# The forward transform over the rows in four 64x64 quarters of TensorE, even and odd rows apart

## The chip, the cores and the metric

The kernel runs on one core of a Trainium2 chip. The metric is the device time of one execution in microseconds; the median of several runs is compared. A profile is one execution recorded by the hardware profiler, with the start and the end of every instruction on each engine: TensorE (PE, with its weight loads as PEld), VectorE (DVE), ScalarE (ACT), GpSimd (POOL) and SyncE (SP), which here only issues transfers. Times within a profile are counted from the start of its span.

## What is computed

```python
x = A_x                                   # 1 x 2048 x 1024
xn = _layernorm(x, axis=-1)
X = rfft2(xn) * (w_r + 1j * w_i)          # w_r, w_i: 2048 x 513
s = irfft2(X, (2048, 1024))
h = silu(einsum("bsd,df->bsf", xn, w1))   # w1: 1024 x 3584
g = silu(einsum("bsf,fd->bsd", h, w2))    # w2: 3584 x 1024
return x + s * g
```

A layer norm feeds two branches. One is a feed-forward layer with two large products. The other multiplies the two-dimensional Fourier transform of the normed rows with a complex filter and transforms back. Both meet in the last line.

## The kernel before

Every product with f32 data is made of three f16 products: each operand is split into a high and a low half, and high x high, high x low and low x high are summed in PSUM.

TensorE has a first stage, the product with w1 (`mm1`, tiles `pa`, 112 groups of 24 matmuls of 512 columns), and a second, the product with w2 (`mm2`, tiles `pb`, 56 groups of 42 in seven combined products, so that fewer are needed than by the plain rule). Between these groups the code puts the matmuls of the Fourier branch:

- `fa` (in `fd_gen`): the transform over the 1024 columns of a row block. VectorE combines its parts (`bfly`), makes four-point sums over four row blocks (`Rb`, `Rd`, `Ro`) and stores the result, split into halves, to the DRAM tensors `vd`.
- `fx` (in `f_gen`): the transform over the 2048 rows s. Before the change it has 16 units u = 4q + j: q is one of four residue classes of the frequency over s, j one of four blocks of 128 column frequencies. `mat(u)` multiplies data `vq` (128 rows, four row classes c, real and imaginary parts) with constants `kq`: for each c and each of the three half products one matmul of 256 columns and two of 128. ScalarE copies half of the sums from PSUM (`xc`), VectorE adds and subtracts (`xb`, `xd`, then `radix4` to `X`), multiplies with the filter (`T`, from the tiles `wq` of w_r and w_i, which ScalarE scales first), makes the first inverse sums (`yb`, `yd`, `Z`), and `high_z` and `low_z` split Z into halves `zq` that go to the DRAM tensors `zd`.
- `iu` and `id` (in `i_gen`): the inverse transforms, on 64-row halves of TensorE. They read `zd` as `zt`.
- The frequencies 0 and 512 over the columns go a way of their own (`xsv`, `edge_gen`, `zp`). `wmax_gen` reads all of w_r and w_i once for a scale `zs`, and `w2max_gen` does so for w2.

The order is written by generators. After each group of the first or second stage `work()` takes a step of the weights' queue `wq`, in three of four cases one of the queue `xq` (the two maxima, then the edge), and up to three steps of the queue `bg`, which holds the Fourier branch: it goes on as long as a model of VectorE's time (`clock`, summed by `meter` from sizes) is no more than `LEAD` = 1 us ahead of that of TensorE. The filter's turn comes when the maxima are done (`switch`). `defer(n, ...)` puts a transfer off by n groups. The order within an engine is fixed by this; the engines run freely against each other and wait on semaphores. SP issues loads (`vq`, `wq`, and the `ht` of the second stage) in one order, POOL's queue the loads of w2 (`jr`) and `kq` and most stores.

PSUM has two buffers for the Fourier branch (pool `pt`, tag `ft`) and four for the large products (`pf`). `vq` and `kq` have two buffers each in the pool of the filter, `xc` has one.

## Time and profile before

| | |
|---|---|
| time, median of 3 runs | 1247.46 us (1245.87 to 1251.45) |
| the profiled execution's own time | 1247.57 us |
| its span | 1245.8 us |
| granted clock of TensorE, mean | 0.997 |
| matmuls, columns transform `fx` | 576, first at 573.3 us, last ones at 810 |
| inverse, `iu` | 768, first at 871.7 us, last at 1150.3 |
| DMA | 296.88 MB, 238 GB/s mean |

A line of the profile's groups reads: source line, engine, operation, the tiles written and read, their shapes, the count, then busy time, mean duration in ns of one, and the engine's idle time just ahead of them with what ended it. A line of the timeline has start and duration in us. A line of the waits has who waited, for whom, the total in us, how often, and the longest. Under DMA stand bytes of one transfer and the median time from issue to landing.

### The profile page before, as it was taken

Reading aid. Unit: us, or ns where it says so; the run is one execution under the profiler, and the core shown is the slowest. Engines: PE = TensorE matmul, PEld = TensorE weight load, DVE = VectorE, ACT = ScalarE, POOL = GpSimd, SP = SyncE. Lnnn points to the kernel's source line nnn. Section 1 sums busy time; section 2 is a strip of 40 time slices with the busy share of each in tenths; the row PEclk is TensorE's granted clock in tenths of the full one; section 3 lists DMA queues with packets and bytes.
Section 4 is the critical chain, followed back from the end, with each engine's and each line's share of the span. In section 5 each row is a group of like instructions: output and inputs, shape, how many; then the busy total and the mean of one; then the engine's idle time right before and its main releaser. Section 6 shows DMA issues by size and latency. Waiting matters only on the chain. (4 is left out here: it accounts for less than half of the span.)

```text
span 1245.8 us, 20664 instructions
## 1 busy us (share of the span) xinstructions
PE 1225.4 (98%) x7759; PEld 621.0 (50%) x7759; DVE 1018.9 (82%) x2056; ACT 499.4 (40%) x672; POOL 321.1 (26%) x526
## 2 busy tenths in 40 slices
PE   8999999999999999999999999999999998999997
...
DVE  6678999998988998565958799894895886895985
...
GB/s 239 124 184 192 126 247 171 192 189 159 156 237 229 236 282 332 254 228 180 196 274 229 264 250 245 295 146 360 234 216 301 207 322 375 248 330 240 231 297 317
DMA packets 161733, 296.88 MB, mean 238 GB/s; under 512 B 32048, under 2 KB 84912, under 8 KB 161120
## 3 DMA queue, kind: packets, MB, share of 16 engines
...
q8 instruction: 61, 1.00, 0.3%
...
q10 hardware_dynamic: 144, 0.13, 0.0%
...
## 5 line engine op out<-in xcount | busy, mean ns | idle before, releaser
L432 PE MATMUL pa<-xnT,w 128*128 128x512 f16 x2688 | 585.1, 379 | 2.6 <-DVE xnT L686 1.7
L432 PEld LDWEIGHTS <-w 128*128 128x128 f16 x2688 | 262.3, 98 | 313.4 <-issue 2.0
L510 PE MATMUL pb<-w,ht 128*128 128x512 f16 (+1 forms) x798 | 300.3, 376 | 0.4 <-DMA ht<-hd_one 0.4
L511 PE MATMUL pb<-w,ht 128*128 128x512 f16 (+1 forms) x798 | 300.0, 376 | 0.0
L512 PE MATMUL pb<-w,ht 128*128 128x512 f16 (+1 forms) x798 | 300.0, 376 | 0.0
L512 PEld LDWEIGHTS <-ht 128*128 128x128 f16 x798 | 78.2, 98 | 91.5 <-issue 0.8
L510 PEld LDWEIGHTS <-ht 128*128 128x128 f16 x798 | 78.3, 98 | 90.3 <-issue 0.8
L511 PEld LDWEIGHTS <-ht 128*128 128x128 f16 x798 | 78.3, 98 | 87.2 <-issue 0.6
L441 ACT ACTIVATE h<-pa,s 128x512 f32<-128x512 f32 x112 | 75.2, 677 | 76.7 <-PE pa L432 70.0
L231 DVE SCALAR_TENSOR_TENSOR w<-jr,sc,w 128x512 f16<-128x512 f32 x98 | 71.9, 745 | 33.9 <-ACT w L228 33.8
L228 ACT ACTIVATE w<-jr,sc 128x512 f16<-128x512 f32 x98 | 68.6, 714 | 76.7 <-DMA jr<-in_B_w_dram 69.6
L388 POOL DMA_DIRECT2D jr<-in_B_w_dram x56 | 36.7, 655 | 226.0 <-issue 162.1
L464 POOL DMA_DIRECT2D hd_sum<-hosum x52 | 38.2, 771 | 183.1 <-DVE hosum L231 116.7
L228 ACT ACTIVATE hosum<-hr,hs 128x1536 f16<-128x1536 f32 x28 | 44.0, 1573 | 88.7 <-DVE hr L471 48.0
L952 ACT ACTIVATE zq<-Z 128x192 f16<-128x192 f32 (+2 forms) x80 | 37.2, 542 | 104.0 <-DVE Z L218 67.4
L228 ACT ACTIVATE hoone<-h,hs 128x2048 f16<-128x2048 f32 x28 | 56.0, 1998 | 53.3 <-DMA hd_one<-hoone 22.7
L231 DVE SCALAR_TENSOR_TENSOR hoone<-h,hs,hoone 128x2048 f16<-128x2048 f32 x28 | 65.6, 2343 | 12.0 <-ACT hoone L228 12.0
L470 DVE TENSOR_TENSOR hr<-h 128x1024 f32<-128x1024 f32 x28 | 34.2, 1220 | 35.3 <-ACT h L441 35.1
L464 POOL DMA_DIRECT2D hd_one<-hoone x52 | 46.0, 884 | 66.1 <-DVE hoone L231 21.1
L231 DVE SCALAR_TENSOR_TENSOR hosum<-hr,hs,hosum 128x1536 f16<-128x1536 f32 x28 | 50.7, 1811 | 3.2 <-ACT hosum L228 3.2
L228 ACT ACTIVATE w<-w1r,rs 128x1024 f16<-128x1024 f32 x28 | 31.8, 1143 | 47.6 <-DVE w L231 26.4
L591 ACT ACTIVATE pl<-pl,c 128x512 f32<-128x512 f32 (+1 forms) x26 | 17.0, 683 | 74.7 <-DVE pl L570 45.6
(215 smaller groups left out, 1798.4 us busy)
## 6 DMA issues: line engine op xcount, KB each, us to landing
jr<-in_B_w_dram POOLq DMA_DIRECT2D x84, 256.0 KB, 7.3
w1r<-in_B_w_dram SPq DMA_DIRECT2D x28, 512.0 KB, 5.9
w2m<-in_B_w_dram SPq DMA_DIRECT2D x28, 512.0 KB, 6.3
...
hd_sum<-hosum POOLq DMA_DIRECT2D x52, 256.0 KB, 4.5
hd_one<-hoone POOLq DMA_DIRECT2D x52, 256.0 KB, 4.5
```

Of the source, the lines that this page charges most:

```text
L228: nc.scalar.activation(hi, raw, AF.Copy, scale=scale)
L231: nc.vector.scalar_tensor_tensor(lo, raw, scale, hi, op0=OP.mult, op1=OP.subtract)
L388: nc.gpsimd.dma_start(raw[n], ws[m][q] if m in ws else w2_block(m, q, 0))
L432: nc.tensor.matmul(ps, w[:, wh, d], xt[:, xh, d], start=(n == 0), stop=(n == 23))
L441: nc.scalar.activation(hq[:, 2 * (c % 2) + f % 2], ps, AF.Silu, scale=s1[:, f:f + 1])
L464: defer(1, lambda k=k, m=m: stores[0].dma_start(hd[m, g][:, :, q].rearrange("f p h s -> f p (h s)"), o[:, k].rearrange("f p h s -> f p (h ...
L470: tt(sums[:, 0:2], hq[:, 0::2], hq[:, 1::2], op=OP.subtract)
L510: nc.tensor.matmul(ps, hh[:, 0], w[:, 0], start=first, stop=False)
L511: nc.tensor.matmul(ps, hh[:, 0], w[:, 1], start=False, stop=False)
L512: nc.tensor.matmul(ps, hh[:, 1], w[:, 0], start=False, stop=last)
L591: nc.scalar.activation(o, o, AF.Silu, scale=c2)
L952: nc.scalar.activation(o[0], z, AF.Copy)
```

## The change

The transform over s now works on the two halves of its symmetric matrix. The residue classes q and q + 2 are taken together (index h), and even and odd rows apart: a unit u has 8 instead of 16 values, and each of its two `mat(u, e)` takes two of the four row classes c. The even rows (b = 0) lie on the first 64 partitions, the odd ones (b = 1) on the others, and each is multiplied with a 64 x 64 block. The four matmuls (b, h) = (0,0), (1,1), (0,1), (1,0) read rows 64b of the array and write columns 64h, so each is one quarter of TensorE, with b in different PSUM banks. `kq` shrinks to half and has one buffer. The sums over even and odd rows, and those between the classes, move to VectorE (`xs`, then two kinds of combination for t = 0 and t = 1, in place of `xb` and `xd` twice).

Column frequencies are sorted by their class of 16 from the first transform on, by the order of the constants `ca` and by the views that `bfly` and the four-point sums use (68 columns for 65 in `bfly`, three more adds per row block in the sums). The split of `Z` then has one or two pieces instead of five and includes the scale `zs`, so ScalarE scales no filter tiles. The filter itself is sorted while `wmax_gen` reads it: five copies on ScalarE for each of 16 blocks, stored to DRAM as `wp` and loaded from there. `zd` is written in 32 stores with runs of 256 bytes. The edge's values take a turn through DRAM (`zpd`).

The queue `xq` gets a step after every group, the edge's loads come 20 groups sooner, and within the filter VectorE's model may be 2 us ahead (`lead`). The diff, cut:

```diff
+    col = np.arange(64)
+    kk = 16 * (col % 4) + col // 4
+    ca = ca[:, :, np.concatenate([kk, 64 + kk])]
...
-    zd = [dp.tile([128, 4, 2, 1024], F16, name=f"zd{c}") for c in range(4)]
...
+    zd = dp.tile([128, 8, 4, 2, 4, 128], F16, name="zd")
...
+    wp = [dp.tile([S, 512], F32, name=f"wp{i}") for i in range(2)]
+    wpv = [t.rearrange("(m2 t m q) k -> q t m m2 k", m2=4, t=2, q=4) for t in wp]
...
-            halves = 2 if name == "pe" and inst.ins[0].ap[0][1] == 64 else 1
+            halves = (2 if inst.ins[0].ap[0][1] == 64 else 1) * (2 if inst.outs[0].ap[0][1] == 64 else 1) if name == "pe" else 1
...
+            for o_, op in ((b, OP.add), (d, OP.subtract)):
+                ov = o_.rearrange("a p r (n l i) -> a n (p r) l i", n=len(parts), i=32)
+                for n, (la, lz, st) in enumerate(parts):
+                    nc.vector.tensor_tensor(ov[:, n], *(rows_[:, k:k + 4, la:lz + 1:st] for k in (0, 4)), op=op)
...
+                t_, o = tl.pop(k - 2), ap.tile([128, 2, 512], F32, name=f"wc{k}", tag="x", bufs=4)
+                nc.vector.tensor_reduce(mt[:, k - 2:k - 1], t_, axis=AX.XY, op=OP.max, apply_absolute_value=True)
+                src = t_.rearrange("m r (i l) -> m r l i", l=16)
+                dst = o.rearrange("m r (g l i) -> m r l g i", g=4, l=4)
+                nc.scalar.activation(o.rearrange("m r (l i) -> m r l i", i=32)[:, :, 0:4], src[:, :, 0:13:4], AF.Copy)
+                for n, (la, st) in enumerate(((3, -1), (13, 1), (5, 1), (11, -1))):
+                    nc.scalar.activation(dst[:, :, n, 1:4], src[:, :, la:la + 3 * st:st], AF.Copy)
+                for i in range(2):
+                    defer(1, lambda o=o, i=i, k=k: stores[0].dma_start(wp[i][128 * k - 256:128 * k - 128, :], o[:, i]))
...
-            t_ = bp.tile([128, 4, 2, 3, 128], F16, name=f"kq{q}", tag="K", bufs=2)
-            nc.gpsimd.dma_start(t_, kf[q])
-            B["k"][q] = t_
+            B["k"][q] = t_ = bp.tile([128, 2, 4, 2, 3, 64], F16, name=f"kq{q}", tag="K", bufs=1)
+            nc.gpsimd.dma_start(t_.rearrange("a p c h t m -> a p (c h t m)"), kf[q])
...
-            t_ = bp.tile([128, 4, 2, 256], F16, name=f"vq{u}", tag="vq", bufs=2)
-            nc.sync.dma_start(t_, vd[j][:, q])
-            B["v"][u] = t_
+            for h in range(2):
+                B["v"][u, h] = t_ = bp.tile([128, 4, 2, 256], F16, name=f"vq{u}_{h}", tag="vq", bufs=2)
+                src = vd[j][:, q + 2 * h].rearrange("(a b) c h k -> b a (c h k)", b=2)
+                for b in range(2):
+                    nc.sync.dma_start(t_[64 * b:64 * b + 64].rearrange("a c h k -> a (c h k)"), src[b])
...
+        def mat(u, e):
+            ps = pt.tile([128, 2, 2, 2, 128], F32, name=f"fx{u}_{e}", tag="ft")
+            k = B["k"][u // 4]
+            for x in range(2):
                 for n, (kh, vh) in enumerate(((0, 0), (0, 1), (1, 0))):
-                    nc.tensor.matmul(o, k[:, c, kh, 1], v[:, c, vh], start=(n == 0), stop=False)
-                    nc.tensor.matmul(ps[:, c, 0], k[:, c, kh, 2], v[:, c, vh, 128:256], start=False, stop=False)
-                    nc.tensor.matmul(ps[:, c, 1], k[:, c, kh, 0], v[:, c, vh, 0:128], start=False, stop=(n == 2))
-            psx[u] = ps
+                    for kind, cols, to in ((1, slice(0, 256), slice(0, 256)), (2, slice(128, 256), slice(0, 128)), (0, slice(0, 128), slice(128, 256))):
+                        for b, h in ((0, 0), (1, 1), (0, 1), (1, 0)):
+                            rows_, out_ = slice(64 * b, 64 * b + 64), slice(64 * h, 64 * h + 64)
+                            o = ps[out_, b, x].rearrange("m r k -> m (r k)")[:, to]
+                            nc.tensor.matmul(o, k[rows_, h, e + 2 * x, kh, kind], B["v"][u, h][rows_, e + 2 * x, vh, cols],
+                                             start=(n == 0 and kind == 1), stop=(n == 2 and kind == 0))
+            psx[u, e] = ps
+
+        def copy(u, e):
+            cps[u, e] = bp.tile([128, 2, 2, 128], F32, name=f"xc{u}_{e}", tag="xc", bufs=2)
...
+            for z, o in by_class(n):
+                stt(o[1], z, zs, o[0], op0=OP.mult, op1=OP.subtract)
+            zs_.pop(n)
+            t_ = zqs.pop(n).rearrange("m h n k -> m (h n) k")
+            for h in range(2):
+                to = zd[64 * t:64 * t + 64, 2 * (q + 2 * h):2 * (q + 2 * h) + 2, :, :, 3 - j].rearrange("m h c r k -> m (h c r) k")
+                defer(1, lambda h=h, to=to: stores[0].dma_start(to, t_[64 * h:64 * h + 64]))
...
+            X = bp.tile([128, 8, 128], F32, name=f"X{n}", tag="X", bufs=2)
+            if n:
+                high_z(n - 1)
+            if t == 0:
+                sd_ = bp.tile([128, 2, 2, 2, 2, 128], F32, name=f"xs{u}", tag="S", bufs=1)
+                for e in range(2):
+                    ps, cpy = psx.pop((u, e))[:, 0], cps.pop((u, e))
+                    for k, op in enumerate((OP.add, OP.subtract)):
+                        tt(sd_[:, k, e], ps, cpy, op=op)
+                if u + 1 < 8:
+                    load_v(u + 1)
+                b = bp.tile([128, 2, 2, 128], F32, name=f"xb{n}", tag="xb", bufs=1)
+                d = bp.tile([128, 2, 2, 128], F32, name=f"xd{n}", tag="xd", bufs=1)
+                tt(b, sd_[:, 0, :, 0], sd_[:, 0, :, 1], op=OP.add)
+                tt(d, sd_[:, 0, :, 0], sd_[:, 0, :, 1], op=OP.subtract)
+                radix4(-1, b, d, X)
+            else:
+                ev = bp.tile([128, 4, 128], F32, name=f"xb{n}", tag="xb", bufs=1)
+                od = bp.tile([128, 4, 128], F32, name=f"xd{n}", tag="xd", bufs=1)
+                pm_ = bp.tile([128, 2, 2, 128], F32, name=f"xp{n}", tag="xp", bufs=1)
+                D = sd_[:, 1]
+                tt(pm_[:, 0], D[:, 1, 0], D[:, 1, 1], op=OP.add)
+                tt(pm_[:, 1], D[:, 1, 0], D[:, 1, 1], op=OP.subtract)
+                tt(ev[:, 0:2], D[:, 0, 0], D[:, 0, 1, ::-1], op=OP.add)
+                tt(ev[:, 2:4], D[:, 0, 0], D[:, 0, 1, ::-1], op=OP.subtract)
+                tt(od[:, 0:2], pm_[:, 1], pm_[:, 0, ::-1], op=OP.add)
+                tt(od[:, 2:4], pm_[:, :, 1], pm_[:, ::-1, 0], op=OP.subtract)
+                b0, b1, d0, d1 = ev[:, 0:4:3], od[:, 0:4:3], ev[:, 2:0:-1], od[:, 1:3]
+                stt(X[:, 0:2], b1, RH, b0, op0=OP.mult, op1=OP.add)
+                stt(X[:, 4:6], b1, -RH, b0, op0=OP.mult, op1=OP.add)
+                stt(X[:, 2:8:5], d1[:, ::-1], RH, d0, op0=OP.mult, op1=OP.add)
+                stt(X[:, 6:2:-3], d1[:, ::-1], -RH, d0, op0=OP.mult, op1=OP.add)
...
+            if u + 1 < 8:
+                mat(u + 1, t)
+                if t and u == 2:
+                    defer(3, lambda: load_k(1))
...
-            if count[0] % 4:
-                slot(xq)
+            slot(xq)
             clock["dve"] = max(clock["dve"], clock["pe"] - 1.0)
             for _ in range(3):
-                if clock["dve"] > clock["pe"] + LEAD or hold[0] or slot(bg) == PAUSE:
+                if clock["dve"] > clock["pe"] + lead[0] or hold[0] or slot(bg) == PAUSE:
...
-            if 44 <= n < 76:
-                load_edge(n - 44)
+            if 24 <= n < 56:
+                load_edge(n - 24)
```

On PE, at the first unit of the filter, before the change; `pa` is a group of the first stage, `kq` the constants and `vq` the data:

```order
L432 MATMUL pa_22_5479<-xnT_670,w_22_4589 128x512
L912 LDWEIGHTS kq_5306
L912 MATMUL fx_5512<-vq_5360,kq_5306 128x256
L913 LDWEIGHTS kq_5306
L913 MATMUL fx_5512<-vq_5360,kq_5306 128x128
L914 LDWEIGHTS kq_5306
L914 MATMUL fx_5512<-vq_5360,kq_5306 128x128
```

And now, where vq_0 and vq_1 are the data of the two classes h, and fx_0 is the tile of e = 0:

```order
L436 MATMUL pa_23_5344<-xnT_490,w_23_4846 128x512
L943 LDWEIGHTS kq_5195
L943 MATMUL fx_0_5375<-vq_0_5232,kq_5195 64x256
L943 LDWEIGHTS kq_5195
L943 MATMUL fx_0_5375<-vq_1_5235,kq_5195 64x256
L943 LDWEIGHTS kq_5195
L943 MATMUL fx_0_5375<-vq_1_5235,kq_5195 64x256
L943 LDWEIGHTS kq_5195
L943 MATMUL fx_0_5375<-vq_0_5232,kq_5195 64x256
L943 LDWEIGHTS kq_5195
L943 MATMUL fx_0_5375<-vq_0_5232,kq_5195 64x128
```

A triple of three full loads and matmuls has become twelve pairs of 64 rows by 64 columns.

On SP, the first loads of the filter, before; `vd` and `w_r`, `w_i` are sources in DRAM:

```order
L892 DMA vq_5434<-vd_76 128x2048
L900 DMA wq_0_5436<-in_A_w_r_dram 64x4x128 x2
L900 DMA wq_1_5439<-in_A_w_i_dram 64x4x128 x2
L892 DMA vq_5551<-vd_77 128x2048
L900 DMA wq_0_5679<-in_A_w_r_dram 64x4x128 x2
L900 DMA wq_1_5682<-in_A_w_i_dram 64x4x128 x2
L892 DMA vq_5699<-vd_78 128x2048
L900 DMA wq_0_5921<-in_A_w_r_dram 64x4x128 x2
L900 DMA wq_1_5924<-in_A_w_i_dram 64x4x128 x2
L892 DMA vq_5934<-vd_75 128x2048
```

And now, from the second filter tile of unit 0 on:

```order
L929 DMA wq_0_5306<-wp_81 64x4x128 x2
L929 DMA wq_1_5309<-wp_82 64x4x128 x2
L921 DMA vq_0_5531<-vd_76 64x2048 x2
L921 DMA vq_1_5534<-vd_76 64x2048 x2
L929 DMA wq_0_5758<-wp_81 64x4x128 x2
L929 DMA wq_1_5761<-wp_82 64x4x128 x2
L929 DMA wq_0_5971<-wp_81 64x4x128 x2
L929 DMA wq_1_5974<-wp_82 64x4x128 x2
L921 DMA vq_0_5986<-vd_77 64x2048 x2
L921 DMA vq_1_5989<-vd_77 64x2048 x2
```

The loads of vq ran two units ahead of their matmuls; now a unit has two tiles of vq, and they are issued when the unit before has been multiplied. On PE, 24 matmuls of `pa` stand between fx_1 of unit 0 and fx_0 of unit 1, 63 or more between the later units, and 84 between unit 3 and unit 4, whose `kq` is the second one. Ahead of the first `fx` stand 2208 matmuls of `pa`, before 2424.

On VectorE, from the sums read out of PSUM to the filter product, one unit, before:

```order
L978 TENSOR_TENSOR xb_6619<-fx_6521,xc_6604 128x512
L979 TENSOR_TENSOR xd_6620<-fx_6521,xc_6604 128x512
L215 TENSOR_TENSOR X_6623<-xb_6619 128x256
L216 TENSOR_TENSOR X_6623<-xb_6619 128x256
L217 TENSOR_TENSOR X_6623<-xd_6620 128x2x128
L218 TENSOR_TENSOR X_6623<-xd_6620 128x2x128
L957 TENSOR_TENSOR zq_6613<-Z_6606,zq_6613 128x8x3x8
L957 TENSOR_TENSOR zq_6613<-Z_6606,zq_6613 128x8x4x8
L957 TENSOR_TENSOR zq_6613<-Z_6606,zq_6613 128x32x8
L957 TENSOR_TENSOR zq_6613<-Z_6606,zq_6613 128x8x3x8
L957 TENSOR_TENSOR zq_6613<-Z_6606,zq_6613 128x8x2x8
L999 TENSOR_TENSOR T_6709<-X_6623,wq_0_6457 128x1024
```

And now:

```order
L1002 TENSOR_TENSOR xs_7542<-fx_0_7210,xc_0_7321 128x512 x2
L1002 TENSOR_TENSOR xs_7542<-fx_1_7386,xc_1_7532 128x512 x2
L1007 TENSOR_TENSOR xb_7553<-xs_7542 128x512
L1008 TENSOR_TENSOR xd_7554<-xs_7542 128x512
L219 TENSOR_TENSOR X_7539<-xb_7553 128x256
L220 TENSOR_TENSOR X_7539<-xb_7553 128x256
L221 TENSOR_TENSOR X_7539<-xd_7554 128x2x128
L222 TENSOR_TENSOR X_7539<-xd_7554 128x2x128
L977 SCALAR_TENSOR_TENSOR zq_7540<-Z_7534,zs,zq_7540 128x1024
L1046 TENSOR_TENSOR T_7656<-X_7539,wq_0_7376 128x1024
L1047 TENSOR_TENSOR T_7658<-X_7539,wq_1_7379 128x1024
```

The second fence is the t = 0 half of a unit now. Ahead of fx_0 of the next unit stand the rows up to X, in the order in which the code was written; its PSUM buffer is the one that the first two xs rows read.

More of the change, by code (lines that the diff above doesn't have):

```diff
@@ L184, in tile_of @@
         return pool.tile(shape, dtype, name=name, tag=tag, bufs=bufs)
-    clock, pace = {"pe": 0.0, "dve": 0.0}, [1.0]
+    clock, pace, lead = {"pe": 0.0, "dve": 0.0}, [1.0], [LEAD]
     COST = {"DVE": ("dve", 0.07, 1.045e-3), "PE": ("pe", 0.0025, 0.4167e-3)}
@@ L837, in fd_gen @@
             o[j] = r.rearrange("a (q r) k -> a q (r k)", r=2)
+            last = j
             yield 3.9
-        high_r(3)
+        high_r(0)
         yield 0.5
-        low_r(3)
+        low_r(0)
         yield 1
@@ L917, in f_gen @@
+        def copy(u, e):
+            cps[u, e] = bp.tile([128, 2, 2, 128], F32, name=f"xc{u}_{e}", tag="xc", bufs=2)
+            nc.scalar.activation(cps[u, e], psx[u, e][:, 1], AF.Copy)
         load_k(0)
-        for n, t_ in enumerate((ones, ident, turn2)):
-            nc.gpsimd.dma_start(t_, pm[:, n])
         yield PAUSE
@@ L964, in f_gen @@
[L964 to L981 removed]
+        tt, stt = nc.vector.tensor_tensor, nc.vector.scalar_tensor_tensor
@@ new lines, in by_class, with high_z @@
+        def by_class(n):
+            src, dst = zs_[n].rearrange("m n (l i) -> m n l i", l=4), zqs[n].rearrange("m h n (l i) -> m h n l i", l=4)
+            for to, k, at in ((0, 4, 0),) if n // 2 % 4 else ((0, 2, 0), (2, 2, 1)):
+                yield src[:, :, at:4:4 // k], [dst[:, h, :, to:to + k] for h in range(2)]
+        def high_z(n):
+            zqs[n] = bp.tile([128, 2, 8, 128], F16, name=f"zq{n}", tag="zq", bufs=2)
+            for z, o in by_class(n):
+                nc.scalar.activation(o[0], z, AF.Copy, scale=zs)
@@ new lines, in f_gen @@
+        mat(0, 0)
+        yield 1
+        mat(0, 1)
+        copy(0, 0)
+        yield 1
+        copy(0, 1)
+        pace[0], lead[0] = 1.05, 2.0
+        for n in range(16):
+            u, t = n // 2, n % 2
+            q, j = u // 4, u % 4
+            X = bp.tile([128, 8, 128], F32, name=f"X{n}", tag="X", bufs=2)
[30 more added lines that the diff above has]
+                stt(X[:, 6:2:-3], d1[:, ::-1], -RH, d0, op0=OP.mult, op1=OP.add)
@@ L982, in f_gen @@
             Xv = X.rearrange("m (a r) k -> m a r k", r=2)
             if j == 0:
-                nc.gpsimd.tensor_copy(xsv[:, 0, q], Xv[:, :, :, 0])
-            if u == 13:
+                nc.gpsimd.tensor_copy(xsv[:, 0, 2 * q + t], Xv[:, :, :, 0])
+            if n == 4:
+                assert w1j.done
+                B["turn2"] = turn2 = bp.tile([128, 128], F32, name="turn2")
+                for k, t_ in enumerate((ones, ident, turn2)):
+                    nc.gpsimd.dma_start(t_, pm[:, k])
@@ L1103, in edge_gen @@
         nc.vector.scalar_tensor_tensor(zpv[:, :, 1], z4, zs, zpv[:, :, 0], op0=OP.mult, op1=OP.subtract)
+        yield 1
+        yield 1
+        to = zpd.rearrange("(t m) q x -> q m t x", t=2)
+        for h in range(2):
+            for q in range(2):
+                g.dma_start(to[q + 2 * h], zp[64 * h:64 * h + 64, 2 * q:2 * q + 2].rearrange("m t c h r -> m t (c h r)"))
+        yield 1
+        yield 1
+        yield 1
+        src = zpd.rearrange("(i b) q x -> b i (q x)", b=2)
+        for b_ in range(2):
+            g.dma_start(zpp[64 * b_:64 * b_ + 64].rearrange("m q c h r -> m (q c h r)"), src[b_])
         yield 1
```

232 lines of the change are left out of this document (93 added, 139 removed).

## The prediction, made before the run

> **What bounds the kernel now.** First the page's busy times, then its slices, then the table of stretches.
>
> ```profile
> PE 1225.4 (98%) x7759; PEld 621.0 (50%) x7759; DVE 1018.9 (82%) x2056; ACT 499.4 (40%) x672; POOL 321.1 (26%) x526
> ...
> PE   8999999999999999999999999999999998999997
> ...
> DVE  6678999998988998565958799894895886895985
> ```
>
> ```profile
> 300.00:400.00 100.00, 100.00 (x539) 48.60 (x538) 92.68 (x202) 49.35 (x62) 40.15 (x60) 1.00 0.62 192
> ...
> 700.00:750.00 50.00, 50.00 (x328) 27.96 (x327) 48.44 (x95) 21.18 (x42) 6.99 (x12) 1.00 0.82 227
> 750.00:800.00 50.00, 48.07 (x319) 26.91 (x317) 49.06 (x91) 20.41 (x38) 11.83 (x27) 1.00 0.99 264
> ```
>
> In the second fence the columns are: stretch, its length, then busy time (and instructions) of PE, PEld, DVE, ACT and POOL, granted clock, DMA share, GB/s. TensorE is busy in every microsecond of nearly every stretch, so a microsecond of its work that goes is a microsecond of span, as long as nothing else makes it stand. But from 700 to 800 us, in the filter, VectorE is busy for 48.4 and 49.1 of 50 us. A busy row alone doesn't say how fast matmuls follow each other, since they overlap; start times do.
>
> **What the forward step costs.** The timeline of TensorE, start and duration in us:
>
> ```profile
> 573.32 0.27 PE L912 MATMUL fx<-vq,kq 128*128 128x256 f16 x1
> 573.43 0.22 PE L913 MATMUL fx<-vq,kq 128*128 128x128 f16 x1
> 573.49 0.22 PE L914 MATMUL fx<-vq,kq 128*128 128x128 f16 x1
> 573.54 0.27 PE L912 MATMUL fx<-vq,kq 128*128 128x256 f16 x1
> ...
> 576.85 0.27 PE L912 MATMUL fx<-vq,kq 128*128 128x256 f16 x1
> ```
>
> From the first to the last row are 16 triples: 3.53 us, so 0.2206 us for one of 256 + 128 + 128 columns. The groups by shape say how many there are:
>
> ```profile
> L912 PE MATMUL fx<-vq,kq 128*128 128x256 f16 x192 | 43.2, 272 | 1.9 <-ACT xc L935 1.9
> ```
>
> 192 triples x 0.2206 = **42.4 us** of TensorE now, and 1.9 us of waiting. The change issues 8 units x 2 halves x 2 rows x 3 terms = 96 triples, each matmul of which is four of 64x64: 1152 pairs of weight load and matmul where 576 stood. No quarter ever ran in this trace, so the cost is bounded by the nearest rows:
>
> ```profile
> 871.71 1.07 PE L1146 MATMUL iu<-kk,zt 64*128 64x128 f16 x32
> ```
>
> ```profile
> 825.82 0.30 PEld L1053 LDWEIGHTS eps<-edge,ident 128*128 128x128 f32 x2
> 826.04 0.30 PEld L1054 LDWEIGHTS eps<-edge,turn 128*128 128x128 f32 x2
> ```
>
> - *Four together.* In the inverse step 32 matmuls on 64-row halves start within 1.07 - 0.22 = 0.85 us, 0.0274 apart, hence 0.055 for two: what one full matmul of 128 columns takes (573.43 to 573.49). Halves already run two at a time without loss. If quarters run four at a time, the step costs 96 x 0.2206 = 21.2 us: **-21.2**.
> - *Pairs issued no faster than there.* That row shows no pair issued closer than 0.0274 us. If this is the instruction stream's own limit, 1152 x 0.0274 = 31.6 us: **-10.8**.
> - *Loads one behind the other.* The edge's matmuls have only 8 columns, so their loads set the pace: two in 826.04 - 825.82, 0.11 us for 128 columns of f32. Half the columns at that rate are 0.055, and 1152 in a row 63.4 us: **+21.0**.
>
> I take the first, because the 64-row halves are the nearest row: smaller tiles that share the array cost nothing there. All three stay in the range.
>
> The Trainium skill speaks against the change in TensorEngine Tiling (Array Packing), Restrictions: column tiling turns fast weight load off. TensorE: Matmul & The Clock Gate, LDWEIGHTS, gives a load as its columns / 1.2 ns, an estimate of 53 ns for 64; by it, one at a time, the sum would be some +19. The edge's loads, 0.11 us for 128 columns, agree with that rate. Its Part 3 says that tiles of different rows overlap; for quarters no run here shows it.
>
> **What the step will wait for.** Three waits are new, and one (1.9, the single xc buffer) goes, since xc has two.
>
> ```profile
> vq<-vd SPq DMA_DIRECT2D x16, 512.0 KB, 7.7
> ...
> kq<-in_kc_dram POOLq DMA_DIRECT2D x4, 768.0 KB, 9.0
> ```
>
> ```profile
> L892 SPq DMA_DIRECT2D vq<-vd x16: 319/544/2052, 540.4 to 792.7; - x16
> ...
> DMA to landing us min/median/max: 3.5/7.7/15.0
> ```
>
> ```profile
> SPq L900 <- DVE T L999: 101.4, 14, 18.2
> ```
>
> ```profile
> POOL jr L388 <- DVE w L231: 73.6, 22, 8.1
> ```
>
> 1. *The vq loads.* Before, a unit's load could go out when the unit two before had been multiplied. Now the next unit needs both buffers, so its four DMAs go out when fx of this unit's second half is done. Behind fx_1 of unit 0 stand 24 matmuls until fx_0 of unit 1:
>
> ```profile
> 26.65 10.52 PE L432 MATMUL pa<-xnT,w 128*128 128x512 f16 x48
> ```
>
> (10.52 - 0.38) / 47 = 0.216 us each, 5.2 us in all. The four loads need some 1.5 us to issue (an issue of vq took 0.32 at least, 0.54 in the middle) and 7.7 to land: about 9, so TensorE stands **4 us**; with landings of 3.5 and 15.0 it is 0 and 11. The six later units have 63 matmuls (13.6 us) or more between: nothing, unless SP is late. It can be, for the wq loads ahead of them wait for T (101.4 us in 14 waits), and behind vq stand the ht loads of the second matmul.
>
> 2. *The constants.* Now one kq buffer: the second load waits for the last fx of unit 3, and unit 4 comes 84 matmuls (18.1 us) later, against 9.0 to land. On POOL it stands behind jr loads, which wait for buffers, 8.1 us at the longest (22 such waits). I take **1 us**; 0 to 8.
>
> 3. *VectorE.* The two PSUM buffers of fx hold the two halves of one unit, so fx_0 of the next unit waits for the first two sums of this one. Before, a unit's buffer had been read a unit earlier. How far VectorE trails TensorE there:
>
> ```profile
> 714.96 0.27 PE L912 MATMUL fx<-vq,kq 128*128 128x256 f16 x1
> ```
>
> ```profile
> 720.29 0.68 DVE L978 TENSOR_TENSOR xb<-fx,xc 128x512 f32<-128x512 f32 x1
> 720.90 0.68 DVE L979 TENSOR_TENSOR xd<-fx,xc 128x512 f32<-128x512 f32 x1
> 721.49 0.41 DVE L215 TENSOR_TENSOR X<-xb 128x256 f32<-128x256 f32 x1
> 721.83 0.42 DVE L216 TENSOR_TENSOR X<-xb 128x256 f32<-128x256 f32 x1
> ...
> 722.83 2.13 DVE L957 TENSOR_TENSOR zq<-Z,zq 128x192 f16<-128x192 f32 x5
> 724.88 1.22 DVE L999 TENSOR_TENSOR T<-X,wq 128x1024 f32<-128x1024 f32 x1
> ```
>
> The program places fx of unit 8 just ahead of that zq group: TensorE is there at 714.96, VectorE at 722.83, 7.9 us later. In the new order two sums (0.6 each by these starts), two more adds of 512 and four of 256 (0.335 each) stand between the awaited sum and zq: 3.7 us. So TensorE would wait 7.9 - 3.7 = **4 us**, once: having stood, it no longer leads. At the unit where it trails most,
>
> ```profile
> 686.99 0.27 PE L912 MATMUL fx<-vq,kq 128*128 128x256 f16 x1
> ```
>
> ```profile
> 699.93 2.14 DVE L957 TENSOR_TENSOR zq<-Z,zq 128x192 f16<-128x192 f32 x5
> ```
>
> 12.9 - 3.7 = 9; where it doesn't trail, 0.
>
> VectorE itself: for two units now 2 x (2 x 0.6 + 4 x 0.335 + 2.05) = 9.2 us in these groups; then six of 512, fourteen of 256 and two zq of 1024, for which a row of the same shape stands:
>
> ```profile
> L822 DVE SCALAR_TENSOR_TENSOR Rs<-Ro,Rs 128x1024 f16<-128x1024 f32 x16 | 19.5, 1219 | 3.4 <-ACT Rs L819 3.4
> ```
>
> 19.5 / 16 = 1.22, in all 10.7. Eight times 1.5 is 12 us more, beside matmuls; if that cover is gone, it is paid in full. The padding of 65 to 68 columns and the split sums of the fourth step add about 4 in the same way. On ScalarE the scaling of wq and most of the zq pieces go, and sorting copies of w come, earlier: nothing, at 40% use. The stores of zd have runs of 256 bytes; 512-byte runs (hd) land in 4.5 us against 5.7 for 2 KB (ws), so I take nothing; only the inverse step, after the filter, reads zd. That the filter starts sooner (2208 first-stage matmuls ahead of it, not 2424) saves no TensorE time by itself.
>
> ```profile
> ws<-wd POOLq DMA_DIRECT2D x42, 256.0 KB, 5.7
> ...
> hd_one<-hoone POOLq DMA_DIRECT2D x52, 256.0 KB, 4.5
> ```
>
> **The sum**, against the profiled execution's 1247.57 (span 1245.8 and 1.77 around it; the median of the runs is 1247.46, so no correction): 1247.6 - 21.2 - 1.9 + 4 + 1 + 4 = 1233.5, say **1234**.
>
> **Rivals.**
> - *Issue-bound quarters* (-10.8). For: twice as many instructions, and no row with closer pairs. Against: the same row is explained by two streams of 128 columns. With waits of 8 (a slower TensorE leads less): 1247.6 - 10.8 - 1.9 + 8 = 1243, no change by the bound below.
> - *Weight loads in a row* (+21.0): the slower side. For: the edge's 0.11 us; against: 64-row halves show full overlap of loads. 1247.6 + 21.0 - 1.9 + 3 = 1270. With 9 us of waits the change turns into a loss where a pair takes over (42.4 + 1.9 - 9) / 1152 = 0.031 us.
> - *Waits eat the gain.* Four together, but waits at their upper ends, 11 + 8 + 9 = 28: 1253. For: DMA share of 0.99 from 750 to 800 us, VectorE at 98%. Against: each wait shortens the next.
>
> **How the numbers follow.** Four together 0.52 (1224 to 1243 by its waits), issue-bound 0.26 (1236 to 1250), loads in a row 0.13 (1260 to 1275), waits eat the gain 0.09 (1244 to 1256). A measurement of this kernel can tell about 0.5%, 6.2 us, from no change: faster is below 1241.2, slower above 1253.7. Faster: 0.52 x 0.95 + 0.26 x 0.35 = 0.59. Slower: 0.13 and half of 0.09, with a little of the second: 0.18. The rest, 0.23, is no change. The range leaves out loads in a row and a little at each end: 1223 to 1256.
>
> **What would show it.** Four together: a triple of quarters starts every 0.22 us, fx blocks of 12 pairs x 6 last 1.3 us and PE's busy time falls by about 21. Issue-bound: pairs 0.027 apart, blocks of 2.0 us. In a row: blocks of 4 us. The waits stand in the idle time ahead of fx: by DMA vq at unit 1, by DMA kq at unit 4, by DVE xs from unit 4 on. I'm wrong if fx waits for xs at every unit, if TensorE waits for ht, or if the span falls by more than the fx blocks do.

## The result, and the profile after

The changed kernel takes **1295.4 us** (1294.3 to 1296.5), the kernel before in the same runs 1246.7: a ratio of 1.039, 95% interval 1.037 to 1.041. The forecast was 1234. The profiled execution took 1296.0 us, with a span of 1294.2.

The page of the changed kernel, busy times and slices:

```profile
PE 1224.3 (95%) x8335; PEld 608.2 (47%) x8335; DVE 1036.2 (80%) x2067; ACT 498.7 (39%) x668; POOL 376.7 (29%) x613
...
PE   8999896869999999999999899999999998999998
...
DVE  7689875869989999869886988882595877989955
```

The full row of nines has holes now, the deepest from the fifth to the ninth slice (130 to 290 us), long before the first `fx`. Busy time hardly fell although half of the `fx` columns went, since matmuls are slower after a hole (below). Three stretches of the changed kernel (length, then busy time and instructions of PE, PEld, DVE, ACT, POOL, granted clock, DMA share, GB/s):

```profile
210.00:220.00 10.00, 6.51 (x23) 2.46 (x22) 3.61 (x3) 4.76 (x7) 3.92 (x6) 0.83 0.53 187
220.00:230.00 10.00, 0.00 (x0) 0.00 (x0) 4.62 (x3) 4.82 (x10) 3.29 (x6) 0.52 0.96 312
230.00:240.00 10.00, 7.71 (x42) 4.62 (x42) 6.95 (x14) 2.81 (x7) 4.04 (x11) 0.62 0.74 238
```

From 220 to 230 us TensorE does nothing, and no other engine is half busy; only the DMA engines are at 0.96. Who TensorE waited for (total us, times, longest):

```profile
PE fa L746 <- ACT L L757: 15.8, 1, 15.8
PE pa L436 <- ACT h L445: 6.4, 3, 2.6
PE fx L943 <- DMA vq<-vd: 6.1, 3, 3.6
PE s L239 <- ACT h L445: 5.9, 1, 5.9
PE iu L1206 <- DVE uw L1217: 5.9, 2, 4.1
PE fx L943 <- DMA kq<-in_kc_dram: 4.8, 1, 4.8
PE pa L436 <- DVE w L235: 4.0, 1, 4.0
```

The largest waits are for ScalarE, at 39% use. Only 10.9 us of the list stand ahead of `fx`.

To compare kernels, I count what TensorE loses: the time from each matmul's start to the next one's, less its columns at full rate (0.216 us for 512, half of that on a half of the array, a quarter on a quarter). This holds idle time and slow clock together. In us, by stretches of the span, with the last matmul's distance from the end of the span:

| | before | after | e15, below |
|---|---|---|---|
| lost, 0 to 150 | 10.5 | 10.4 | 10.5 |
| 150 to 300 | 0.4 | 42.1 | 0.0 |
| 300 to 520 | 0 | 0 | 0 |
| 520 to 850 (filter) | 2.9 | 20.6 | 5.2 |
| 850 to the end (inverse step) | 12.4 | 23.3 | 14.7 |
| `fx` at full rate | 42.4 | 21.2 | 21.2 |
| end of the span after the last matmul's start | 7.7 | 6.3 | 9.0 |

After less before: -21.2 for `fx`, +41.7, +17.7, +10.9 and -1.4 make 47.7; the spans differ by 48.4.

**The quarters do what was forecast.** One block of the changed kernel, 72 pairs, on TensorE:

```profile
670.08 1.52 PE L943 MATMUL fx<-vq,kq 64*64 64x256 f16 x72
```

The last pair ends 0.22 after its start, so the pairs start within 1.30 us: 6 triples x 0.2206 is 1.32. Every block that follows no wait reads so.

**The first hole.** ScalarE of the changed kernel (start, duration; in brackets the idle time ahead and what ended it), where `wc` is the sorted copy of a block of the filter:

```profile
175.93 0.64 ACT L877 ACTIVATE wc<-wm 128x256 f32<-128x256 f32 x1 [6.25 <-issue]
...
205.06 0.65 ACT L877 ACTIVATE wc<-wm 128x256 f32<-128x256 f32 x1
205.60 1.79 ACT L879 ACTIVATE wc<-wm 128x192 f32<-128x192 f32 x4
...
212.84 0.64 ACT L877 ACTIVATE wc<-wm 128x256 f32<-128x256 f32 x1 [3.41 <-DMA wp<-wc]
...
220.76 0.63 ACT L877 ACTIVATE wc<-wm 128x256 f32<-128x256 f32 x1 [3.16 <-DMA wp<-wc]
...
228.99 0.63 ACT L877 ACTIVATE wc<-wm 128x256 f32<-128x256 f32 x1 [4.42 <-DMA wp<-wc]
229.52 1.75 ACT L879 ACTIVATE wc<-wm 128x192 f32<-128x192 f32 x4
...
231.66 0.57 ACT L757 ACTIVATE L<-fa 128x504 f32<-128x504 f32 x1
232.13 0.68 ACT L445 ACTIVATE h<-pa,s 128x512 f32<-128x512 f32 x1
...
281.14 0.64 ACT L877 ACTIVATE wc<-wm 128x256 f32<-128x256 f32 x1 [5.52 <-issue]
```

and the stores on POOL's queue:

```profile
207.69 1.10 POOL L881 DMA_DIRECT2D wp<-wc  x2 [7.15 <-ACT wc L879]
...
215.43 1.07 POOL L881 DMA_DIRECT2D wp<-wc  x2 [6.01 <-ACT wc L879]
```

A copy waits until the store of the copy just before it has landed: the copies at 212.84 and 220.76 begin some 5 us after the issues at 207.69 and 215.43, and 0.14 us after those stores land (212.70 and 220.62). From the second copy to the fourteenth all but the one at 205.06 begin so. The stores of these copies go out 0.3 us after the end of the copy in most cases and 1.1 at the most, so they don't stand behind other work on POOL's queue. `wm` and `wc` share four buffers; three hold blocks being loaded or read, so one is left for `wc`. Its turn is 2.4 us of sorting, the issue, and the landing: 7.7 us at best (175.93 to 183.67), and (281.14 - 175.93) / 12 = 8.8 on average from the second copy to the fourteenth. One block belongs to each group of 5.2 us. In ScalarE's order `L` (the evacuation of `fa`) and `h` stand behind the waiting copy: they start at 231.66 and 232.13, right after the copies at 229.52. Until then PSUM isn't freed, and TensorE takes over the pace of one buffer.

**Slow clock behind the longer holes.** TensorE of the changed kernel, `fa` ahead of the hole and behind it, and `pa` behind a shorter one:

```profile
204.18 0.22 PE L748 MATMUL fa<-cas,xnT 128*128 128x128 f16 x1
204.23 0.22 PE L746 MATMUL fa<-cas,xnT 128*128 128x128 f16 x1
...
209.49 7.03 PE L436 MATMUL pa<-xnT,w 128*128 128x512 f16 x24 [2.58 <-ACT h L445]
...
232.45 0.31 PE L748 MATMUL fa<-cas,xnT 128*128 128x128 f16 x1
232.56 0.31 PE L746 MATMUL fa<-cas,xnT 128*128 128x128 f16 x1
```

The same matmuls start 0.056 us apart before, 0.107 after: half the rate, for some 5 us; the granted clock from 232.3 to 237.4 us is 0.50. 24 matmuls take 7.03 us behind a stand of 2.58, where 23 x 0.216 + 0.38 = 5.35 is usual. So a stand of 2.6 to 5 us costs here some 1.7 to 3 us more than itself.

### The profile page after: what moved, and what is told of

Its sections match the earlier page's. It is cut to its first block, busy times and chain, and to the rows that moved or that the text cites. A ratio compares the mean times of both kernels' runs of the same rounds, so it can differ in the third digit from the quotient of the medians.

```text
span 1294.2 us, 22000 instructions
## 1 busy us (share of the span) xinstructions
PE 1224.3 (95%) x8335; PEld 608.2 (47%) x8335; DVE 1036.2 (80%) x2067; ACT 498.7 (39%) x668; POOL 376.7 (29%) x613
## 4 chain that ended last, share of the span: by engine, by line
PE 47%; DVE 14%; DMA 11%; ACT 2%; issue 2%; SPq 2%; POOL 1%; DVEq 0%; ACTq 0%; POOLq 0%
PE pa L436 26%; PE pb L514 6%; PE pb L515 6%; PE pb L516 6%; DMA pl<-pd 4%; DMA ht<-hd_dif 2%; PE fx L943 2%; DMA fs<-sd 1%; DVE us L1236 1%; DMA kq<-in_kc_dram 1%; ACT us L1235 1%; DMA out_dram<-pl 1%; DMA vq<-vd 1%; DMA ht<-hd_sum 1%; DVE uw L1216 1%
## 5 line engine op out<-in xcount | busy, mean ns | idle before, releaser
L436 PE MATMUL pa<-xnT,w 128*128 128x512 f16 x2688 | 594.7, 383 | 12.8 <-ACT h L445 6.4
L235 DVE SCALAR_TENSOR_TENSOR hoone<-h,hs,hoone 128x2048 f16<-128x2048 f32 x28 | 65.6, 2343 | 10.4 <-ACT hoone L232 10.3
L474 DVE TENSOR_TENSOR hr<-h 128x1024 f32<-128x1024 f32 x28 | 34.2, 1220 | 33.7 <-ACT h L445 33.4
L232 ACT ACTIVATE w<-w1r,rs 128x1024 f16<-128x1024 f32 x28 | 31.9, 1142 | 54.0 <-DVE w L235 24.7
L830 DVE SCALAR_TENSOR_TENSOR Rs<-Ro,Rs 128x1024 f16<-128x1024 f32 x16 | 19.5, 1219 | 32.9 <-ACT Rs L827 32.9
```

The lines of the kernel that those rows point to most:

```text
L232: nc.scalar.activation(hi, raw, AF.Copy, scale=scale)
L235: nc.vector.scalar_tensor_tensor(lo, raw, scale, hi, op0=OP.mult, op1=OP.subtract)
L436: nc.tensor.matmul(ps, w[:, wh, d], xt[:, xh, d], start=(n == 0), stop=(n == 23))
L474: tt(sums[:, 0:2], hq[:, 0::2], hq[:, 1::2], op=OP.subtract)
L830: nc.vector.scalar_tensor_tensor(sp[j][:, :, 1], o[j], 2.0**-21, sp[j][:, :, 0], op0=OP.mult, op1=OP.subtract)
```

## The experiments

All times below are medians; the ratio is to the kernel before in the same runs (1245.8 to 1247.6 us). The last two columns are read from the one profiled execution of each kernel, which lies up to 4.2 us from the median (e13: 1246.6).

| run | us | ratio, 95% interval | lost 150-300, 300-520, 520-850, 850-end | end after last matmul |
|---|---|---|---|---|
| e1_two_slots | 1274.4 | 1.022 (1.020 to 1.024) | 11.9, 8.5, 17.6, 23.8 | 6.3 |
| e2_three_of_four | 1277.1 | 1.024 (1.022 to 1.026) | 8.2, 0, 22.4, 31.9 | 10.9 |
| e3_loads_first | 1283.8 | 1.029 (1.027 to 1.031) | 42.0, 0, 6.7, 24.0 | 6.8 |
| e4_both | 1265.5 | 1.015 (1.013 to 1.017) | 11.9, 8.6, 6.4, 27.8 | 6.8 |
| e5_models | 1301.3 | 1.043 (1.041 to 1.045) | 32.3, 12.0, 34.2, 11.7 | 7.1 |
| e6_two_paced | 1273.7 | 1.021 (1.019 to 1.022) | 5.7, 4.3, 11.2, 34.9 | 13.2 |
| e7_all | 1261.0 | 1.010 (1.009 to 1.012) | 7.2, 0, 9.5, 18.0 | 19.8 |
| e8_all_keep_lead | 1269.4 | 1.018 (1.016 to 1.019) | 7.5, 0, 9.6, 37.0 | 10.5 |
| e9_early11 | 1254.5 | 1.007 (1.005 to 1.009) | 0.1, 0, 10.1, 20.9 | 18.5 |
| e10_seven_of_eight | 1249.3 | 1.003 (1.001 to 1.004) | 6.6, 5.0, 15.5, 11.2 | 9.0 |
| e11_every_group | 1262.6 | 1.013 (1.011 to 1.015) | 10.5, 12.9, 15.1, 11.3 | 8.0 |
| e12_lead14 | 1262.2 | 1.013 (1.011 to 1.015) | 1.4, 0, 9.7, 29.1 | 18.9 |
| e13_later_unit1 | 1242.4 | 0.996 (0.995 to 0.998) | 6.7, 5.1, 4.2, 18.2 | 8.7 |
| e14_five_of_six | 1240.8 | 0.995 (0.993 to 0.997) | 6.6, 4.5, 5.9, 13.1 | 9.1 |
| **e15_four_of_five** | **1232.5** | **0.989 (0.987 to 0.991)** | 0, 0, 5.2, 14.7 | 9.0 |
| e16_quarter_by_quarter | 1320.5 | 1.059 (1.056 to 1.062) | 39.2, 0.4, 44.8, 29.9 | 6.3 |

### The sorted copy's buffer, and its pace

e1 loads one block ahead instead of two, which leaves two buffers for `wc`:

```diff
-        for k in range(18):
+        for k in range(17):
...
-            if k >= 2:
-                t_, o = tl.pop(k - 2), ap.tile([128, 2, 512], F32, name=f"wc{k}", tag="x", bufs=4)
+            if k >= 1:
+                t_, o = tl.pop(k - 1), ap.tile([128, 2, 512], F32, name=f"wc{k}", tag="x", bufs=4)
```

> The filter's blocks (wm) are loaded one block ahead instead of two, so the sorted copy (wc) gets two of the four shared buffers instead of one; the same copies, stores and numbers. Theory S (a loop through one buffer: 2.4 us of sorting on ScalarE, then 5.4 us until the store has landed, 7.8 us per block where a group of TensorE lasts 5.2; ScalarE stands in order, so PSUM isn't freed): the waits of ACT wc for DMA wp go from 32.6 us to under 5, the losses of 23 + 13 us between 200 and 300 us go, 1259 us (1255 to 1266). Theory C (38 us of copies in 16 groups are too much for ScalarE whatever the buffers): h stays late, TensorE still stands, 1285 to 1296. Theory Q (the stores stand behind others on POOL's queue): between, 1270 to 1285.

Measured: 21 us faster than the change, not 36. The same copies cost 30 us less between 150 and 300 us, so the loop through one buffer carries most of that loss, and ScalarE's added work alone doesn't explain it. The time itself lies where theory Q had it, but Q is out, since the stores of the changed kernel go out right behind their copies (above). What ScalarE waited for ahead of `wc` in e1 (us, times):

```profile
  ACT wc L879: 25.7, 9
  DMA wm<-in_A_w_i_dram: 8.2, 2
  issue: 7.4, 3
  DMA wp<-wc: 3.5, 2
```

The wait for the store is 3.5 us, where it was 32.6. A new one has come, for the block itself, now loaded later, behind other loads on SP, and it holds up the same queue:

```profile
218.34 0.64 ACT L877 ACTIVATE wc<-wm 128x256 f32<-128x256 f32 x1 [7.24 <-DMA wm<-in_A_w_i_dram]
```

e2 leaves the buffers and steps the queue of the maxima in three of four groups, as the kernel before did:

```diff
-            slot(xq)
+            if count[0] % 4:
+                slot(xq)
```

> The changed kernel with the queue of the maxima stepped in three of four groups again, nothing else. A block then comes every 6.9 us on average. Theory S: the loop of 7.8 us is still longer than that, 0.9 us x 16 = 14 us of loss instead of 42, 1267 us (1258 to 1275), and ACT wc still waits for DMA wp. Theory C: 38 us of copies spread over 21 groups leave ScalarE free enough, 1253 to 1258, with the waits for DMA wp unchanged in number. If the pace has nothing to do with it: 1290 or more.

Measured: between 150 and 300 us 8.2 are left, of which 6.6 are another stand, at 161 us. That is less than theory S gave (14): a block then comes every 6.9 us, the copies fall behind by under 1 us each, and the four PSUM buffers of `pa`, three groups or 15 us of slack, can hold that; that they do is my reading, not measured by itself. The time is 10 us worse than expected: the filter, now with 2328 matmuls of `pa` ahead of it instead of 2208, meets new waits (`vq` 14.9 us, and 31.9 us lost in the inverse step).

### The loads of the filter

e3 issues a unit's `vq` loads right behind the product that frees their buffers, and the second `kq` there too, on SP:

```diff
-                if u + 1 < 8:
-                    load_v(u + 1)
...
-                if t and u == 2:
-                    defer(3, lambda: load_k(1))
+                if t and u == 2:
+                    load_k(1, nc.sync)
+                if t and u + 2 < 8:
+                    load_v(u + 2)
```

(The first two units' loads are issued ahead of the loop.) In the change SP stands in order ahead of those loads; its queue, from the timeline:

```profile
579.81 24.80 SPq L929 DMA_DIRECT2D wq<-wp  x8
604.70 3.88 SPq L921 DMA_DIRECT2D vq<-vd  x4
```

The products on TensorE that free the buffers, the second ones of units 1 and 3:

```profile
595.23 1.52 PE L943 MATMUL fx<-vq,kq 64*64 64x256 f16 x72
...
705.96 1.52 PE L943 MATMUL fx<-vq,kq 64*64 64x256 f16 x72
```

`vq` of unit 2 could go out at 597, but stood until 604.7 behind `wq` loads that waited for `T`. `kq` could go out at 707.5; POOL issued it 11 us later:

```profile
718.43 0.71 POOL L913 DMA_DIRECT2D kq<-in_kc_dram  x1
```

> The changed kernel with the vq loads of a unit issued right behind the product that frees their buffers (ahead of the wq loads that wait for T on SP), and the second kq load there too, on SP instead of POOL three groups later. Theory O (the waits of fx for vq and kq come from the order of issue): idle of 6.1 + 4.8 us ahead of fx goes to under 2, and the slow clock behind each wait (3 us each) goes with it, 1279 us (1275 to 1285). Rival (the transfers themselves are late at a DMA share of 0.8 to 1.0, or what now stands behind them on SP, the ht loads, is late instead): gain under 5 us, 1290 or more, with new waits of pb for ht.

Measured: 20.6 us lost in the filter became 6.7, the rest stayed as it was, and the time fell by 11.5. Theory O holds, somewhat smaller than forecast.

e4 is e1 and e3 together.

> The two edits of the first and the third run together (two slots for the sorted copy, loads issued first). If the losses are separate they add: 1296 - 36 - 16 = 1244 us (1238 to 1250), the kernel before being at 1247, and what is left over the -21 of fx is the wait of 6 us near 160 us and 11 us in the inverse step. If a shared limit stands behind both (VectorE late, or the filter begun sooner collides with the second stage): 1255 or more.

Measured 1265.5, 21 us above the sum: not so much because the two edits meet (the gains measured in e1 and e3 alone add up to 1262.9), but because each left something. The first stage still loses 11.9 and 8.6 us (copies that wait for `wm`), the inverse step 27.8.

### The model's lead, and the inverse step

The change lets VectorE's model run 2 us ahead (`lead`) in the filter, and doesn't set it back behind it: it holds for the inverse step too. e5 sets it back, and gives 1.5 us to the first row block:

```diff
+        lead[0] = 1.5 if c == 0 else LEAD
...
-        pace[0] = 1.0
+        pace[0], lead[0] = 1.0, LEAD
```

> The changed kernel with two constants of the order alone: VectorE's model may be 1.5 us ahead instead of 1 while the first row block is transformed (so the Rs piece comes ahead of hoone on ScalarE again, as in the kernel before), and the 2 us that the filter allows are set back to 1 behind it. Theory R (the stand of 4.0 us at 161 us comes from Rs standing behind hoone on ScalarE): it goes, -6 us with its slow clock. Theory L (the inverse step loses 11 us more than before because VectorE's orders may now be 2 us ahead, so TensorE meets sums that aren't done): waits of iu and id for uw, us and sw fall from some 15 to 7 us, -10 us. Both: 1280 us (1276 to 1286). If the inverse step's waits have another cause (the step lies elsewhere against the second stage): -6 alone, 1289.

Measured: slower, 1301. In its stretch theory L holds, 23.3 us lost in the inverse step became 11.7. But the filter now begins where its loads meet other work (`fx` waits 16.6 us for `vq` and 6.2 for `xs`), and of the stand at 161 us 3.2 of 4.0 us of idle time are left: theory R fell in this form.

e6 is e4 with the maxima in three of four groups; e7 adds the two constants of e5; e8 is e7 without setting the lead back.

> Two slots for the sorted copy, loads issued first, and the maxima in three of four groups. In e4_both TensorE still loses some 13 us between 220 and 450 us, where fa waits for its evacuation, which stands on ScalarE behind a sorting copy that waits for wm to land. Theory S in its wider form (a copy that waits for a transfer, whichever, holds up ScalarE): with 1.7 us more per block it is ready in time, 1266 - 13 = 1253 us (1248 to 1257). Theory C (ScalarE's added work): the same loss comes at another place, 1260 or more.

> All of it: two slots, loads issued first, the maxima in three of four groups, and the two constants of e5. If the parts add: 1253 - 6 (the stand at 161 us) - 10 (inverse step) = 1237 us (1230 to 1245), faster than the kernel before by the rest of the 21 us that fx saves. If the filter's later end collides with the inverse step: 1247 or more, with waits in the last 200 us.

> As e7_all, but the 2 us of lead stay on behind the filter, as in the change. Theory L: 8 to 12 us slower than e7_all, in waits of iu and id. If the lead has nothing to do with those waits: the same as e7_all within 3 us.

Measured: in e6 the first stage's loss is nearly gone (5.7 and 4.3), as the wider theory S has it, but 34.9 are lost in the inverse step, 20 us over the expectation. e7 and e8 part by 8.4 us, as theory L expects. TensorE's waits in e8:

```profile
PE id L1250 <- DVE sw L1259: 16.6, 3, 13.0
PE id L1250 <- ACT us L1237: 5.8, 2, 5.7
```

and in e7:

```profile
PE id L1250 <- ACT us L1237: 2.5, 2, 1.6
...
PE id L1250 <- DVE sw L1259: 2.2, 2, 1.5
```

With 2 us of lead, `id` is placed ahead of sums that VectorE hasn't finished. But e7 is 24 us above its expectation, and not on TensorE, whose last matmul starts at 1236.1, 2 us earlier than in the kernel before. The last stretch of e7:

```profile
1230.00:1255.80 25.80, 6.34 (x59) 5.44 (x56) 17.30 (x42) 4.39 (x9) 0.00 (x0) 0.66 0.67 236
```

TensorE is done and VectorE isn't: the inverse step's last `id` starts at 1217.8, 34 us later than before the change, and the output waits for it.

### The stand at 161 us, and when the filter begins

In the kernel before, the split of `w` follows `hosum` on VectorE:

```profile
151.86 1.81 DVE L231 SCALAR_TENSOR_TENSOR hosum<-hr,hs,hosum 128x1536 f16<-128x1536 f32 x1
156.10 1.28 DVE L231 SCALAR_TENSOR_TENSOR w<-w1r,rs,w 128x1024 f16<-128x1024 f32 x1 [2.43 <-ACT w L228]
```

In the changed kernel a piece of the transform (`Rs`) stands ahead of that split, and VectorE waits for its other half, which ScalarE makes only after `hoone`:

```profile
157.24 1.23 DVE L830 SCALAR_TENSOR_TENSOR Rs<-Ro,Rs 128x1024 f16<-128x1024 f32 x1 [5.90 <-ACT Rs L827]
...
159.85 1.28 DVE L235 SCALAR_TENSOR_TENSOR w<-w1r,rs,w 128x1024 f16<-128x1024 f32 x1
```

In e7 a piece of `Rs` still waits there for ScalarE, ahead of the split for which TensorE waits:

```profile
157.44 1.23 DVE L831 SCALAR_TENSOR_TENSOR Rs<-Ro,Rs 128x1024 f16<-128x1024 f32 x1 [1.22 <-ACT Rs L828]
...
160.05 1.28 DVE L235 SCALAR_TENSOR_TENSOR w<-w1r,rs,w 128x1024 f16<-128x1024 f32 x1
```

e9 is e7 with a lead of 1.1 in the first row block, which gives back the earlier order at that place:

```diff
-        lead[0] = 1.5 if c == 0 else LEAD
+        lead[0] = 1.1 if c == 0 else LEAD
```

> As e7_all, with 1.1 instead of 1.5 us of lead in the first row block, so that the first Rs piece comes ahead of hoone and the second one behind the split of w that TensorE waits for, both as in the kernel before. Theory R': the stand at 161 us (4.3 us, 7.0 with the slow clock) comes from a Rs piece standing on VectorE ahead of the split of w, and goes: 1254 us (1250 to 1258). If the widened sums (68 columns, copies of V) make VectorE late there whatever the order: 1261 as before, the stand unchanged.

Measured as expected: 1254.5, and 0.1 us lost between 150 and 300. Theory R' holds: one piece placed a group later or earlier was 6 to 7 us.

e10 and e11 step the maxima in seven of eight and in all groups (`count[0] % 8`, or no condition); e12 is e9 with a lead of 1.4 in the inverse step.

> As e9_early11, with the maxima in seven of eight groups: the filter begins some 3 groups (16 us) sooner. Theory T (in e7_all TensorE ends at 1236, 2 us before that of the kernel before, but the span ends 20 us later than that, since the chain through VectorE, filter and inverse step, ends 34 us later than before): the tail of 20 us shrinks by some 10, and no copy waits yet: 1244 us (1238 to 1250). Rival (the copies wait again at this pace): stands between 200 and 450 us, 1254 or more.

> As e9_early11, with the maxima in every group, as in the change: the filter begins 30 us sooner than in e9_early11. Theory T: no tail left (7 us as in the kernel before), but fa waits for its evacuation behind copies that wait for wm, 13 us between 220 and 450 us: 1250 us (1243 to 1256). If the tail has another cause than the filter's begin, it stays at 15 to 20 us: 1262.

> As e9_early11, with a lead of 1.4 instead of 1 us in the inverse step (the change has 2). The lead is an exchange: with 2 (e8_all_keep_lead) TensorE stands 25 us there for sums that aren't done and the tail is 10.5 us, with 1 (e7_all) it stands 8 and the tail is 20. Between them I expect 12 us of stands and a tail of 15: the same as e9_early11 within 4 us. If one of the large stands (13 us) comes at once: 5 us or more slower.

Measured: e10 begins the filter at 527.1 instead of 546.6 us, and its tail is 9.0 us where e9 has 18.5. Its last `id` starts at 1185.0 instead of 1214.0, so the tail comes from when the filter begins (theory T); but TensorE itself ends 7 us later than in e9, and the time falls by only 5. What is left in e10 has names: 11.6 us behind copies that wait, and 10.5 at unit 1, where `fx` waits 8.4 for `vq`. In e11 the copies' waits take more than expected (23 us) and put the filter off again, to 538.8. In e12 stands came back without the tail getting shorter: the lead is no free exchange.

### Down to the single waits

e13 is e10 with the first product of unit 1 two groups later:

```diff
+            if n == 0:
+                yield PAUSE
+                yield PAUSE
             if u + 1 < 8:
                 mat(u + 1, t)
```

e14 and e15 step the maxima in five of six and four of five groups (`count[0] % 6`, `% 5`).

> As e10_seven_of_eight, with the first product of unit 1 put two groups (10 us) later. There TensorE stands 6.7 + 1.7 us for vq, 10.5 us with the slow clock, since only one group lies between the product that frees the buffers and the one that needs them. Theory W (what is left over the kernel before are waits, each with its place): 1249 - 10 = 1239 us (1235 to 1245). Theory V (VectorE's longer chain through filter and inverse step sets the end, so what TensorE gains comes back as a tail): 1248 or more, the tail grows from 9 towards 18 us.

> As e13_later_unit1, with the maxima in five of six groups. In e10 some 11 us are lost between 200 and 415 us behind copies that wait; at three of four groups none are. Theory W: 3 to 8 us less loss there, 1235 us (1230 to 1242). Theory V: the filter begins 2 groups later and the tail takes it back, 1246 or more.

> As e13_later_unit1, with the maxima in four of five groups, between e14 and the three of four of e9_early11 (tail 18.5 us). Theory W: the same as e14 within 4 us. Theory V: slower than e14 by 5 us or more, with a tail of 14 to 18 us.

Measured: 1242.4, 1240.8 and 1232.5. Theory V fell: no tail is over 9.1 us. Theory W holds, though its guess of the best pace did not: at five of six, 11 us are lost in the first stage as at seven of eight, at four of five none, and the filter begins as early (526.3 us, against 528.0 in e13). e15 is 1.1% faster than the kernel before, and faster than the changed kernel. Its page:

```profile
PE 1206.0 (98%) x8335; PEld 600.6 (49%) x8335; DVE 1034.6 (84%) x2067; ACT 497.7 (40%) x668; POOL 373.1 (30%) x612
...
PE   8999999999999999999999999999999999999997
```

and TensorE's longest waits:

```profile
PE id L1253 <- DVE sw L1262: 4.9, 3, 2.4
PE tp L682 <- ACT x L673: 2.2, 3, 1.1
```

PE's busy time is 19.4 us under that of the kernel before: the saving of `fx`, visible once no hole slows the rest.

### What makes four quarters run together

e16 is the change with the nine matmuls of one quarter one after another, in place of the four quarters in turn:

```diff
-                for n, (kh, vh) in enumerate(((0, 0), (0, 1), (1, 0))):
...
-                        for b, h in ((0, 0), (1, 1), (0, 1), (1, 0)):
+                for b, h in ((0, 0), (1, 1), (0, 1), (1, 0)):
+                    for n, (kh, vh) in enumerate(((0, 0), (0, 1), (1, 0))):
```

> The changed kernel with the same matmuls of fx in another order: the nine of one quarter of TensorE one after another, then those of the next quarter, instead of the four quarters in turn. If four quarters run together only where they stand next to each other in the instruction stream, a block of 72 pairs lasts 24 triples x 0.22 = 5.3 us instead of 1.30, and the time is up to 16 x 4 = 64 us longer (1340 to 1365). If TensorE looks ahead past the instructions of one quarter, blocks stay at 1.3 to 2 us and the time at 1295 to 1305.

One block of e16:

```profile
598.09 3.76 PE L943 MATMUL fx<-vq,kq 64*64 64x256 f16 x72
```

Measured: starts spread over 3.54 us, between the two expectations. 16 x (3.54 - 1.30) = 36 us more of TensorE (in the table most of its 44.8 us of loss), 25 us more of time. The order of the instructions is part of the gain. Why it is 3.54, and not 5.3, is open, and so is whether rows or columns decide: in turn, each matmul reads another row half than the one ahead of it, in e16 only every ninth does.

## Why the prediction was wrong

By its own steps:

- **The bound**: right. TensorE's starts set the span before and after, and in e15 what `fx` saves arrives.
- **Four together**, -21.2: right, blocks of 1.30 us as named. Both rivals on the quarters, issue-bound and loads in a row, are out for this order. The Trainium skill's rule that spoke against it (TensorEngine Tiling (Array Packing), Restrictions: column tiling turns fast weight load off) didn't decide here: 72 pairs in 1.30 us are 0.018 us per pair, while one load of `kq` lasts 0.107 in the profile (median). So the loads overlap. By the Trainium skill's TensorE: Matmul & The Clock Gate, LDWEIGHTS, a load of 64 columns is an estimated 53 ns, three times the 0.018.
- **The xc wait**, -1.9: right, it is gone.
- **vq**, +4: 6.1 us of idle time, 9.8 with the slow clock, but at another place. At unit 1 it was 1.05; the rest came at unit 2, from SP behind `wq` loads, which the text named ("unless SP is late") and priced at nothing.
- **kq**, +1: 4.8, and 7.7 with the slow clock. The text counted from the last `fx` of unit 3; the load is deferred by three groups and stood behind `jr` on POOL, so it went out 11 us later, and landed after 12, not 9.
- **VectorE's lag**, +4: 0, and 0 in e15 too, where TensorE had not stood ahead of the filter; of all the runs only e5 shows such a wait (`fx` for `xs`, 6.2). Why it doesn't come otherwise is open. VectorE's added work was right (12 + 4 forecast, 17.3 measured). That it lies beside matmuls held only as long as the filter begins early: at three of four groups a tail of 18 to 20 us came of it (e7, e9).
- **ScalarE at nothing**: "the scaling of wq and most of the zq pieces go, and sorting copies of w come, earlier: nothing, at 40% use". **This step failed**, with 36 of the 62 us. A share of use doesn't price work on an engine that takes its work in order and waits for transfers. What had to be priced was the loop of the copy: 7.7 to 8.8 us through one buffer against a group of 5.2, and who stands behind it. The other 6 of the first stage's 42 us are the `Rs` piece at 161 us, a moved step whose order was not followed up.
- **The inverse step** had no term at all; the lead that stays at 2 us cost some 11. The prediction, and the text on the change, took it to end with the filter.
- **The slow clock** had no term either. The trace of before had one sign of it, a granted clock of 0.97 from 1050 to 1100 us, where TensorE stood 2.4 us. The Trainium skill has it in TensorE: Matmul & The Clock Gate, Part 1 (half the clock after an idle window of about 3.4 us). Here stands of 2.6 us already brought it, and one of 2.0 in e13.

Forecast 1233.5, profile 1296.0: of the 62.5 us, 42 are the first stage, 11 the filter's waits beyond those priced, 11 the inverse step, less 1 at the end. No rival held this; the one that came closest in time, loads in a row (1270), is wrong in its mechanism, and "waits eat the gain" looked only at the filter. That e15 comes to 1232.5, next to the forecast, is in part luck. The -21.2 is the same, but with its loads issued first and unit 1 put later the filter loses 2.3 us more than before, where the forecast had a net 7.1, and the inverse step and the end cost 3.6 that the forecast didn't have.

What stays open: the lead's effect was measured on kernels with other edits too (e7 against e8), and in the change itself only as a loss in one stretch (e5). Theory C, ScalarE's work by itself, was not tried with the copies left out; but e9 and e15 make the same 80 copies and lose 0.1 us or less between 150 and 520 us, so this work costs TensorE next to nothing once its buffers and its pace fit.
